# From the sixth chunk on, the second feed-forward product as seven block products, with streamed sums of weight blocks

## The chip, the core and the metric

One Trainium2 chip, one of its cores. A core has a matrix engine (TensorE, "PE" in the profile; its weight loads are listed apart as "PEld"), a vector engine (VectorE, "DVE"), a scalar engine (ScalarE, "ACT"), GpSimd ("POOL") and SyncE ("SP"), whose queue issues every transfer of this kernel. Working data lies in SBUF, on 128 partitions; products land in PSUM, which this kernel cuts into eight banks of 512 float32 columns. The metric is the device time of one launch in microseconds, here the median of three runs.

## The reference, cut to what matters

```python
# attention: q, k, v are (8 batches, 8 heads, 576, 64); 32 landmarks per head
q_lm, k_lm = means of q, k over 18 neighbouring rows
A, Bm, C = softmax(q k_lm'), softmax(q_lm k_lm'), softmax(q_lm k')
Z = inverse of Bm by six Newton steps
x = (A @ Z @ C @ v), heads side by side          # (8, 576, 512)
# feed-forward
u  = x + real(fft(fft(x, axis=1), axis=2))
un = (u - mean(u)) / sqrt(var(u) + 1e-6)         # per row of 512
out = u + np.maximum(un @ w_ch1, 0.0) @ w_ch2    # w_ch1 (512, 2048), w_ch2 (2048, 512)
```

The change touches the last product, `h @ w_ch2` with `h = max(un @ w_ch1, 0)`, for 8 x 576 = 4608 rows.

## The kernel before, in words

**Numbers in two halves.** Every large operand is split into a float16 high part and a float16 low part, "hi" and "lo". `mm3` makes one product of such pairs from three matmuls that add up in PSUM: hi x hi, hi x lo, lo x hi.

**Tiles and chunks.** The 4608 rows are 36 tiles of 128 rows. Attention works through eight batches; `mix` makes the tiles of a batch (four, or five with a tile shared by two batches), `norm` normalizes them, splits them and has them transposed by DMA into a buffer `unT`, which holds two tiles. Two tiles (256 rows) form a chunk, so there are 18 chunks, numbered 0 to 17. Tile `u` stays in a buffer of its own until its chunk is finished.

**A chunk** (`chunk`) loops over eight pairs of blocks of 128 hidden units; the prediction calls one such pass a group. In each group,
- the first product fills a bank `hp` with two blocks x 256 rows: 2 x 4 x 3 = 24 matmuls of 256 columns, stationary operand from `w1s`;
- ACT writes `h` hi as the ReLU of the bank, and DVE writes `h` lo;
- the second product adds to two banks `acc`, one per tile of 128 rows: 2 x 2 x 3 = 12 matmuls of 512 columns, stationary operand `h`, moving operand `w2s` (both weights stay in SBUF).

After the eighth group, DVE adds each `acc`, scaled by `inv2`, to its `u`, and SP stores `u`.

**The order of the work.** Operations are not issued as the Python code meets them. `Order` collects them with their dependences; `solve` plays them through with a price for each operation and writes an order for each engine. Among the operations that are ready and whose buffers are free, an engine takes the one with the lowest phase (`set`): -1 for the operations that turn `hp` into `h` and for the end of a chunk, 100 x the batch for attention, 1000 for the second product, 1001 for the first. So the first product fills PE's time when nothing else is ready. Consecutive matmuls between `together` and `apart` are one entry. A consumer on PE is planned a margin later than its operand is (0.8 us for the second product). On the chip each engine follows its list and waits on semaphores; each list is strictly in order, SP's too.

**Buffers** are pools with a number of slots, and those in `IN_ORDER` are given out in program order. The ones that matter are

```python
BANKS = {"at": 4, "h": 2, "acc": 2}
SLOTS = {"big": (1280, 8), ..., "u": (512, 7), "unT": (1024, 3), "h": (512, 4), "ws": (512, 3)}
```

(columns of float32, number of slots). `at` are attention's PSUM banks; `big` holds a batch's loads of q, k and v and its large intermediates; `ws` is a float32 work buffer of `weights`, which scales and splits both weights at the start.

In the profile nearly every operation has the line of the helper that issues them (1039), so operations are told apart by tile names: `hp<-unT,w` is the first product, `acc<-w,h` the second, `h<-hp` the ReLU and the low part, `u<-acc` the end of a chunk, `at<-...` attention's products, `big<-k_dram` a load, `unT<-row` a transposing DMA.

Of the kernel before, what the change touches and what calls it, by code (L numbers as in the profile page):

```python
# [10 lines left out]
F32 = mybir.dt.float32  # L11
F16 = mybir.dt.float16
# [3 lines left out]
AF = mybir.ActivationFunctionType  # L16
ALU = mybir.AluOpType
# [66 lines left out]
BANKS = {"at": 4, "h": 2, "acc": 2}  # L84
SLOTS = {"big": (1280, 8), "ml": (640, 3), "mt": (512, 5), "row": (528, 6), "u": (512, 7), "unT": (1024, 3), "h": (512, 4), "ws": (512, 3)}
# [20 lines left out]
class View:  # L106
# [42 lines left out]
    def box(self):  # L149
        if self.at_psum():  # L150
# [211 lines left out]
class Kernel:  # L362
    def __init__(self, ctx, tc, NB, q, k, v, w1, w2, t1, t1t, t2, diag, mask, out):
# [3 lines left out]
        pool = lambda n: ctx.enter_context(tc.tile_pool(name=n, bufs=1))  # L367
        self.pool, self.sm = pool("sb"), {}
        self.ps = ctx.enter_context(tc.tile_pool(name="ps", bufs=1, space=bass.MemoryType.PSUM))
        self.order = Order()  # L370
# [148 lines left out]
    def weights(self):  # L519
# [5 lines left out]
        s1, e1, s2, inv = (self.kept([P, n], F32, name) for n, name in ((4, "wsa"), (4, "wea"), (4, "wsb"), (1, "winv")))  # L525
        self.inv2 = inv
        for w in range(2):
            gram = self.new("acc")
            for f in range(NF):
# [3 lines left out]
                top, low = rv[:, :, 1], rv[:, :, 0]  # L533
                dst, mag = slots[w][f], low.bitcast(F32) if w else self.new("h")
                x = dst.bitcast(I32)
# [23 lines left out]
                if w == 0:  # L559
                    V.reciprocal(e1[:, g : g + 1], r)  # L560
                    V.tensor_scalar(s1[:, g : g + 1], r, 2.0**12, None, ALU.mult)
                else:
                    least = self.small(1, "wleast")
                    V.tensor_tensor(r, r, s1, ALU.mult)
                    V.tensor_reduce(least, r, AX.X, ALU.min)
                    V.tensor_scalar(s2, e1, least, 4.0, ALU.mult, ALU.mult)
                    V.reciprocal(inv, least)
                    V.tensor_scalar(inv, inv, 2.0**-13, None, ALU.mult)
                for f2 in range(NF) if w else range(4 * g, 4 * g + 4):
                    src, (hi, lo) = self.new("ws"), (hl[w][f2][:, y] for y in range(2))  # L570
# [8 lines left out]
    def load(self, b):  # L579
        res = []  # L580
        for g in range(2):
            kf, qf = self.big(), self.big()
            gs = slice(2 * g, 2 * g + 2)
            self.dma(kf[:, 0 : 2 * S].rearrange("p (r t) -> p r t", r=2), self.k[b, :, gs])
            self.dma(qf[:, 0 : 16 * SEG].rearrange("p (r t) -> p r t", r=2), self.q[b, :, gs])
            res.append([kf, qf])
        for g in range(2):
            vf = self.big()
            self.dma(vf.rearrange("p (c d) -> p c d", c=5), self.v[b, g].rearrange("(c p) d -> p c d", p=P))
            res[g].append(vf)  # L590
        return res

    def attention(self, b):
# [3 lines left out]
        self.set(10 * b if b == 0 else 100 * b, b, 0.1 if b == 0 else 0.4 if b == 1 else 1.0)  # L597
        loads = self.load(b)
        if b == 0:
            self.later()  # L600
# [36 lines left out]
        for g in range(2):  # L637
            qs = loads[g][1][:, 0:NQ].rearrange("p (x t) -> p x t", t=2 * SEG)
            for t, a, w in ((qm[g], 1, 128), (qr[g], 129, 16)):
                split(  # L640
                    *(t[:, y].rearrange("p r (s t) -> p (r s) t", t=w) for y in range(2)),
                    qs[:, :, a : a + w], sc[:, g : g + 1],
                )
        scr = self.small(1, "scr")
        for g in range(2):
# [77 lines left out]
    def landmarks(self, b, loads, qbd, lm):  # L723
# [84 lines left out]
        for g in range(2):  # L808
# [7 lines left out]
            A.copy(ET[:, 0:4].rearrange("p t m -> p (t m)"), ps)  # L816
            ps = self.at()
            tr(ps[:64, 0:128], Ces[g][:, 512:576], self.ident)
            A.copy(ET[:64, 4], ps[:64, 0:128])
# [27 lines left out]
        for g in range(2):  # L847
            for i in blocks:
                mm(ps[i, 64 * g : 64 * g + 64], nrm[i, g, 0, :], RE[i, g, 32:])
            for i, rows in enumerate(blocks):  # L850
                o, r = i % 2, i // 2
# [133 lines left out]
    def chunk(self, ch):  # L985
# [4 lines left out]
        for i in range(NF // 2):  # L990
            self.set(1001, -1, 0.3)
            ps = self.new("hp")
            for x in range(2):
# [4 lines left out]
                self.apart()  # L998
            if ch == 0 and i < 4:
                t = self.mid(512)  # L1000
            else:
                t = self.new("h")
            h = t.bitcast(F16).rearrange("p (y x t) -> p y x t", y=2, x=2)
# [13 lines left out]
        for t in range(TCH):  # L1017
            u = self.utiles[TCH * ch + t]
            V.scalar_tensor_tensor(u, acc[t], self.inv2, u, ALU.mult, ALU.add)
            self.dma(self.out[(TCH * ch + t) * P : (TCH * ch + t + 1) * P, :], u)  # L1020

    def run(self):
        self.ntile, self.utiles, self.unT = 0, [], []
        chunks = 0
        for b in range(self.NB):
# [81 lines left out]
```

## Time and profile before

| | |
|---|---|
| runs | 1051.32, 1051.76, 1053.48 us; median 1051.76 us |
| profiled execution | 1050.58 us; its span, first to last instruction, 1048.4 us |
| mean granted TensorE clock | 0.974 |
| PE busy | 982.3 us of the span |
| DVE, ACT, POOL busy | 592.7, 341.8, 191.7 us |
| first product | 3456 matmuls of 256 columns |
| second product | 1728 matmuls of 512 columns by the code, of which the trace recorded 1680 with `h` as the operand and 48 of chunk 0 with `mt` |
| chunk 4 ends, chunk 5 ends | stores begin at 417.15 and 460.14 us |

Rows of groups read: line, engine, operation, output<-inputs, shapes, xcount | busy us, mean ns of one | idle time of the engine just before, and who ended it. Rows of the timeline read: start us, length us, engine, what, xcount merged, and the idle time before with its releaser in brackets. Rows of stretches give the busy time of each engine, in brackets the instructions, then the granted clock, the share of the DMA engines and GB/s. Matmuls overlap, so the mean length of a matmul is not the time that it costs; distances between starts are.

### The profile page before, as it was taken

Reading aid. Unit: us, or ns where it says so; the run is one execution under the profiler, and the core shown is the slowest. Engines: PE = TensorE matmul, PEld = TensorE weight load, DVE = VectorE, ACT = ScalarE, POOL = GpSimd, SP = SyncE. Lnnn points to the kernel's source line nnn. Section 1 sums busy time; section 2 is a strip of 40 time slices with the busy share of each in tenths; the row PEclk is TensorE's granted clock in tenths of the full one; section 3 lists DMA queues with packets and bytes.
Section 4 is the critical chain, followed back from the end, with each engine's and each line's share of the span. In section 5 each row is a group of like instructions: output and inputs, shape, how many; then the busy total and the mean of one; then the engine's idle time right before and its main releaser. Section 6 shows DMA issues by size and latency. Waiting matters only on the chain.

```text
span 1048.4 us, 21403 instructions
## 1 busy us (share of the span) xinstructions
PE 982.3 (94%) x8922; PEld 665.0 (63%) x8922; DVE 592.7 (57%) x1558; ACT 341.8 (33%) x749; POOL 191.7 (18%) x199
## 2 busy tenths in 40 slices
PE   4664879999999999999999999999999999999998
PEld 3444735666666666766676676667666666667674
DVE  6999997995968752246744774178415243131111
ACT  4567553453524431123421442045212121111110
POOL 2458443033122100101110221021102000010000
PEclk9686989999999999999999999999999999999999
DMA  9656402325015200115110501051111100020000
GB/s 343 197 198 183 137 1 51 135 52 184 12 45 162 36 11 11 31 31 172 27 29 26 167 14 41 21 160 26 42 31 21 32 1 26 16 51 21 1 21 21
DMA packets 90992, 72.99 MB, mean 70 GB/s; under 512 B 61328, under 2 KB 79760, under 8 KB 90768
## 3 DMA queue, kind: packets, MB, share of 16 engines
q1 hardware_dynamic: 90896, 71.63, 22.4%
q8 instruction: 70, 1.15, 0.4%
q14 instruction: 26, 0.21, 0.1%
HBM read 48.02 MB, written 9.44 MB: 55 GB/s over the span
## 4 chain that ended last, share of the span: by engine, by line
PE 78%; DVE 16%; issue 2%; ACT 2%; POOL 1%; DMA 1%; SPq 0%; DVEq 0%; ACTq 0%; POOLq 0%
PE acc L1039 33%; PE hp L1039 32%; PE at L1039 13%; DVE w L1039 4%; DVE row L1039 2%; DVE big L1039 1%; DVE u L1039 1%; DVE ws L1039 1%; DVE Wx L1039 1%; DVE mt L1039 1%; DVE h L1039 1%; ACT Wx L1039 1%; DVE lm L1039 1%; DVE cmx L1039 1%; DMA big<-q_dram 1%
## 5 line engine op out<-in xcount | busy, mean ns | idle before, releaser
L1039 PE MATMUL hp<-unT,w 128*128 128x256 f16 x3456 | 400.7, 273 | 0.2 <-DVE h L1039 0.2
L1039 PEld LDWEIGHTS <-w 128*128 128x128 f16 (+1 forms) x3584 | 343.8, 98 | 81.0 <-DVE w L1039 19.2
L1039 PE MATMUL acc<-w,h 128*128 128x512 f16 x1680 | 384.2, 380 | 1.0 <-ACT h L1039 0.7
L1039 PEld LDWEIGHTS <-h 128*128 128x128 f16 x1680 | 160.4, 98 | 182.0 <-issue 6.3
L1039 DVE SCALAR_TENSOR_TENSOR h<-hp,h 128x512 f16<-128x512 f32 x140 | 96.4, 688 | 294.5 <-ACT h L1039 293.8
L1039 ACT ACTIVATE h<-hp 128x512 f16<-128x512 f32 x140 | 83.5, 596 | 387.4 <-PE hp L1039 378.9
L1039 POOL TENSOR_TENSOR r<-ve,mhalf 128x2 f32<-128x2 f32 (+1 forms) x20 | 14.4, 718 | 419.6 <-DVE ve L1039 397.9
L1039 DVE SCALAR_TENSOR_TENSOR u<-at,scw,row 128x128 f32<-128x128 f32 (+3 forms) x120 | 39.4, 387 | 32.2 <-PE at L1039 32.0
L1039 POOL TENSOR_TENSOR row<-row,row 128x512 f16<-128x512 f32 x36 | 45.1, 1265 | 38.8 <-ACT row L1039 38.8
L1039 PEld LDWEIGHTS <-mt 128*128 128x128 f16 x432 | 38.3, 100 | 17.8 <-issue 8.8
L1039 PEld LDWEIGHTS <-big 128*128 128x128 f16 (+1 forms) x768 | 40.4, 104 | 12.5 <-issue 6.5
L1039 DVE TENSOR_REDUCE lm<-big 128x32 f32<-128x576 f32 (+1 forms) x48 | 44.1, 942 | 5.9 <-DMA big<-k_dram 5.0
L1039 POOL TENSOR_TENSOR mt<-mt,asum 128x512 f32<-128x512 f32 x14 | 14.5, 1047 | 165.0 <-DVE asum L1039 163.7
L1039 POOL TENSOR_TENSOR w<-ws,w 128x512 f16<-128x512 f32 x24 | 33.0, 1392 | 18.3 <-ACT w L1039 18.3
L1039 DVE SCALAR_TENSOR_TENSOR u<-acc,winv,u 128x512 f32<-128x512 f32 x36 | 27.0, 750 | 14.7 <-PE acc L1039 14.7
L1039 PE MATMUL at<-big,qbd 128*64 128x288 f32 x128 | 22.5, 481 | 12.1 <-DVE qbd L1039 11.7
L1039 ACT ACTIVATE big<-big 128x1168 f16<-128x1168 f32 (+1 forms) x26 | 25.5, 984 | 25.5 <-DMA big<-q_dram 13.8
L1039 PE MATMUL at<-ml,big 128*128 128x262 f16 (+1 forms) x288 | 32.3, 284 | 0.7 <-DVE u L1039 0.6
L1039 ACT CAST row<-row 128x512 f16<-128x512 f32 x36 | 21.6, 616 | 32.4 <-DVE row L1039 26.3
L1039 DVE TENSOR_TENSOR mt<-mt 128x256 f32<-128x256 f32 x48 | 28.4, 609 | 5.7 <-PE at L1039 3.6
L1039 PE MATMUL acc<-w 128*128 128x128 bf16 x128 | 13.7, 245 | 19.0 <-DVE w L1039 16.4
L1039 PE MATMUL at<-RE 32*32 32x96 f32 (+1 forms) x768 | 26.2, 254 | 5.6 <-DVE RE L1039 5.6
(165 smaller groups left out, 982.1 us busy)
## 6 DMA issues: line engine op xcount, KB each, us to landing
w<-w_dram SPq DMA_DIRECT2D x22, 512.0 KB, 5.6
big<-v_dram SPq DMA_DIRECT2D x16, 640.0 KB, 9.2
big<-q_dram SPq DMA_DIRECT2D x16, 584.0 KB, 6.2
big<-k_dram SPq DMA_DIRECT2D x16, 576.0 KB, 4.8
out_dram<-u SPq DMA_DIRECT2D x36, 256.0 KB, 2.0
big<-w_dram SPq DMA_DIRECT2D x10, 512.0 KB, 6.9
unT<-row SPq DMA_TRANSPOSE x72, 2.4
t<-t_dram SPq DMA_DIRECT2D x1, 1048.0 KB, 9.9
```

The lines of the kernel that those rows point to most:

```text
L1039: getattr(engine, name)(*map(real, args), **{k: real(x) for k, x in kw.items()})
```

## The change

Chunks 0 to 4 stay as they are; chunks 5 to 17 (13 of 18) go through a new function `seven`.

In a group the second product multiplies a block matrix of 2 x 2 (two tiles of rows by two blocks of hidden units, each 128 x 128) with one of 2 x 2 (two blocks of hidden units by two halves of 256 output columns). `chunk` takes eight block products for that; `seven` takes Strassen's seven, each on sums or differences of blocks of both sides.

- *Left factors.* ACT writes the ReLU as float32 into `r` (a `ws` buffer). Two of the seven factors are blocks of `r` themselves: ACT copies their high parts to `h`, DVE subtracts for the low parts. The other five are sums and differences, made by three DVE operations into `c` (a new pool `sum`, 2 slots); ACT copies the high parts of all five (640 columns) to `h`, and POOL subtracts for the low parts (640 columns). `h` grows to 896 columns and has 3 slots.
- *Right factors.* Four of the seven are kept in SBUF: b11 and b22 as they were, and b12 - b22 and b21 - b11, which are written over b12 and b21 after chunk 4 (`differences_of`). Three (b11 + b22, b11 + b12, b21 + b22) are made once after chunk 3 (`sums_of`, 24 blocks), stored to device memory as 128 KB each, and loaded again in every group of every later chunk: 3 loads a group, 312 in all, into a ring of ten places in two `big` buffers that are held to the end.
- *Products.* Seven `mm3` of 256 columns, 21 matmuls instead of 12 of 512. The seven sums go to seven half banks: the two `acc` and two banks that are taken from `at` and held to the end.
- *End of a chunk.* DVE puts the seven sums together into the two `u`: two operations of 512 columns and eight of 256, instead of two of 512.
- *Room for it.* `unT` has 2 slots instead of 3. From the third batch on (`LATE`) v is loaded after the high and low parts of q are made. One bundle of attention's matmuls is cut in two, and the claim of `ET` is repeated for its second part, so that two `at` banks suffice. The scales of the weights are halved and doubled, so that sums of blocks stay in range.

```diff
-SLOTS = {"big": (1280, 8), ..., "unT": (1024, 3), "h": (512, 4), "ws": (512, 3)}
-IN_ORDER = ("big", "ml", "mt", "unT", "h", "ws", "hp", "acc")
+SLOTS = {"big": (1280, 8), ..., "unT": (1024, 2), "h": (896, 3), "ws": (512, 3), "sum": (640, 2)}
+IN_ORDER = ("big", "ml", "mt", "unT", "h", "ws", "sum", "hp", "acc")
+SEVEN, RING, LATE = 5, 10, 2
...
+    def block(self, n, a, b, op, out=None):
+        add = (self.G if n % 2 else self.V).tensor_tensor
+        t = self.new("ws")
+        add(t.rearrange("p (y d) -> p y d", y=2), a, b, op)
+        x = t[:, 0:256]
+        add(x, x, t[:, 256:512], ALU.add)
+        hl = t[:, 256:512].bitcast(F16).rearrange("p (y d) -> p y d", y=2) if out is None else out
+        self.A.copy(hl[:, 0], x)
+        self.G.tensor_tensor(hl[:, 1], x, hl[:, 0], ALU.subtract)
+        if out is None:
+            m = self.dram.tile([P, 256], F32, name=f"sums{len(self.sums)}")
...
+            self.dma(self.sums[-1], t[:, 256:512])
...
+    def seven(self, ch):
...
+        if ch == SEVEN:
+            self.held_banks = [self.new("at") for _ in range(2)]
+            self.ring = [self.new("big") for _ in range(2)]
...
+        acc = [self.new("acc") for t in range(TCH)] + self.held_banks
+        half = lambda k: acc[k // 2][:, 256 * (k % 2) : 256 * (k % 2) + 256]
+        for i in range(NF // 2):
+            (b11, b12), (b21, b22) = self.halves(i)
+            units = []
+            self.set(1000, -1)
+            for j in range(3):
...
+                self.dma(to, self.sums[3 * i + j])
...
+            self.set(1001, -1, 0.3)
+            ps = self.new("hp")
...
+            self.set(-1, -1)
+            r, c = self.new("ws"), self.new("sum")
+            h = self.new("h").bitcast(F16).rearrange("p (y k t) -> p y k t", y=2, k=7)
+            A.activation(r, ps, AF.Relu)
+            ones = r.rearrange("p (k t) -> p k t", k=4)[:, 0:4:3]
+            A.copy(h[:, 0, 0:2], ones)
+            rx = r.rearrange("p (x u t) -> p x u t", x=2, u=2)
+            V.tensor_tensor(c[:, 0:256], r[:, 0:256], r[:, 256:512], ALU.add)
+            V.tensor_tensor(c[:, 256:512].rearrange("p (x t) -> p x t", x=2), rx[:, :, 1], rx[:, :, 0], ALU.subtract)
+            V.tensor_tensor(c[:, 512:640], r[:, 0:128], r[:, 384:512], ALU.add)
+            V.tensor_tensor(h[:, 1, 0:2], ones, h[:, 0, 0:2], ALU.subtract)
+            cv = c.rearrange("p (k t) -> p k t", k=5)
+            A.copy(h[:, 0, 2:7], cv)
+            G.tensor_tensor(h[:, 1, 2:7], cv, h[:, 0, 2:7], ALU.subtract)
+            self.set(1000, -1, 0.8)
+            for to, k, w in ((0, 1, b21), (1, 0, b12), (2, 2, b22), (3, 3, b11), (6, 4, units[1]), (5, 5, units[2]), (4, 6, units[0])):
+                self.together()
+                mm3(half(to), lambda y: h[:, y, k], lambda y: w[:, y], start=(i == 0 and to in (0, 2, 5, 6)), stop=(i == NF // 2 - 1))
+                self.apart()
+        self.set(-1, -1)
+        u0, u1 = self.utiles[TCH * ch : TCH * ch + 2]
+        for u in (u0, u1):
+            V.scalar_tensor_tensor(u, acc[0], self.inv2, u, ALU.mult, ALU.add)
+        for k, plus, less in ((2, (u0, 1), (u0, 0)), (3, (u1, 0), (u1, 1)), (6, (u1, 1), None), (5, None, (u0, 0)), (4, (u0, 0), None), (4, (u1, 1), None)):
+            for to, scale in ((plus, self.inv2), (less, self.ninv2)):
+                if to:
+                    part = to[0][:, 256 * to[1] : 256 * to[1] + 256]
+                    V.scalar_tensor_tensor(part, half(k), scale, part, ALU.mult, ALU.add)
...
     def run(self):
...
-                self.chunk(chunks)
+                (self.seven if chunks >= SEVEN else self.chunk)(chunks)
                 chunks += 1
+                if chunks == SEVEN - 1:
+                    for i in range(NF // 2):
+                        self.sums_of(i)
+                elif chunks == SEVEN:
+                    for i in range(NF // 2):
+                        self.differences_of(i)
```

More of the change, by code (lines that the diff above doesn't have):

```diff
@@ L84 @@
 BANKS = {"at": 4, "h": 2, "acc": 2}
-SLOTS = {"big": (1280, 8), "ml": (640, 3), "mt": (512, 5), "row": (528, 6), "u": (512, 7), "unT": (1024, 3), "h": (512, 4), "ws": (512, 3)}
-IN_ORDER = ("big", "ml", "mt", "unT", "h", "ws", "hp", "acc")
+SLOTS = {"big": (1280, 8), "ml": (640, 3), "mt": (512, 5), "row": (528, 6), "u": (512, 7), "unT": (1024, 2), "h": (896, 3), "ws": (512, 3), "sum": (640, 2)}
+IN_ORDER = ("big", "ml", "mt", "unT", "h", "ws", "sum", "hp", "acc")
 LINK, PATIENCE = 0.05, 0.0
+SEVEN, RING, LATE = 5, 10, 2
 XP, LP = ((1, 1, 1, 1), (1, 1, 1, 1)), ((1, 1, 1, 1), (1, 0, 1, 0))
@@ L149, in box @@
     def box(self):
-        if self.at_psum():
+        if self.ap.space in (bass.MemoryType.PSUM, bass.MemoryType.DRAM):
             return 0, P, 0, 1 << 20
@@ L533, in weights @@
                 top, low = rv[:, :, 1], rv[:, :, 0]
-                dst, mag = slots[w][f], low.bitcast(F32) if w else self.new("h")
+                dst, mag = slots[w][f], low.bitcast(F32) if w else self.new("h")[:, 0:512]
                 x = dst.bitcast(I32)
@@ L586, in load, with load_v @@
             res.append([kf, qf])
+        return res
+    def load_v(self, b, loads):
         for g in range(2):
@@ L589, in load @@
             self.dma(vf.rearrange("p (c d) -> p c d", c=5), self.v[b, g].rearrange("(c p) d -> p c d", p=P))
[L590 to L591 removed]
+            loads[g].append(vf)
     def attention(self, b):
@@ L598, in attention @@
         loads = self.load(b)
+        if b < LATE:
+            self.load_v(b, loads)
         if b == 0:
@@ L643, in attention @@
                 )
+        if b >= LATE:
+            self.load_v(b, loads)
         scr = self.small(1, "scr")
@@ L817, in landmarks @@
             ps = self.at()
+            self.order.claim(ET)
             tr(ps[:64, 0:128], Ces[g][:, 512:576], self.ident)
@@ L849, in landmarks @@
                 mm(ps[i, 64 * g : 64 * g + 64], nrm[i, g, 0, :], RE[i, g, 32:])
+        self.apart()
+        self.together()
+        for g in range(2):
             for i, rows in enumerate(blocks):
@@ L998, in chunk @@
                 self.apart()
[L999 to L1002, printed above, removed]
+            t = self.mid(512) if ch == 0 and i < 4 else self.new("h")[:, 0:512]
             h = t.bitcast(F16).rearrange("p (y x t) -> p y x t", y=2, x=2)
@@ L1020, in chunk, with halves @@
             self.dma(self.out[(TCH * ch + t) * P : (TCH * ch + t + 1) * P, :], u)
+    def halves(self, i):
+        return [[self.w2s[2 * i + x][:, :, 256 * d : 256 * d + 256] for d in range(2)] for x in range(2)]
+    def block(self, n, a, b, op, out=None):
[9 more added lines that the diff above has]
+            m = self.dram.tile([P, 256], F32, name=f"sums{len(self.sums)}")
+            tile_ = Tile(Pool([m], False, kept=True))
+            tile_.slot = 0
+            self.sums.append(View(tile_, m))
+            self.dma(self.sums[-1], t[:, 256:512])
@@ L1022, in run @@
     def run(self):
+        self.unit, self.sums = 0, []
         self.ntile, self.utiles, self.unT = 0, [], []
```

36 lines of the change are left out of this document (33 added, 3 removed).

## The prediction

> **What bounds the kernel now.** I read the page first: busy times, then the chain that ended last.
>
> ```profile
> span 1048.4 us, 21403 instructions
> ...
> PE 982.3 (94%) x8922; PEld 665.0 (63%) x8922; DVE 592.7 (57%) x1558; ACT 341.8 (33%) x749; POOL 191.7 (18%) x199
> ...
> GB/s 343 197 198 183 137 1 51 135 52 184 12 45 162 36 11 11 31 31 172 27 29 26 167 14 41 21 160 26 42 31 21 32 1 26 16 51 21 1 21 21
> ...
> PE 78%; DVE 16%; issue 2%; ACT 2%; POOL 1%; DMA 1%; SPq 0%; DVEq 0%; ACTq 0%; POOLq 0%
> ```
>
> PE carries 78% of the chain, but a share over the whole span mixes stages. The view of stretches cuts it at 417 us, where the fifth chunk ends (chunk 4, counted from 0) and the changed ones would begin, and at 925 us, where attention is over.
>
> ```profile
> core 0: us, PE busy (x) PEld busy (x) DVE busy (x) ACT busy (x) POOL busy (x), PEclk, DMA share, GB/s
> 100.00:417.00 317.00, 302.98 (x3160) 203.38 (x3158) 238.31 (x648) 133.11 (x305) 75.51 (x77) 0.98 0.25 72
> 417.00:925.00 508.00, 507.68 (x4379) 344.67 (x4378) 241.37 (x651) 134.79 (x294) 62.87 (x65) 1.00 0.17 49
> 925.00:1003.00 78.00, 78.00 (x547) 53.28 (x545) 15.68 (x29) 10.79 (x18) 3.09 (x3) 1.00 0.07 18
> ```
>
> From 417 us on PE is idle for 0.3 us of 508, at a granted clock of 1.00; DVE works 241 of 508. What the change touches is a stage where only PE sets the time, so matmul time taken out there is worth its full length, as long as PE stays fed. The busy PE need not be PE at its best rate, so I take rates from the chain in time order, between starts in the pure feed-forward tail, and the weight loads from the groups of that stretch:
>
> ```profile
> 996.58 5.24 PE hp L1039 x48
> 1001.82 5.18 PE acc L1039 x24
> ```
> ```profile
> L1039 PEld LDWEIGHTS <-w 128*128 128x128 f16 x643 | 62.9, 98 | 10.3
> L1039 PEld LDWEIGHTS <-h 128*128 128x128 f16 x320 | 31.3, 98 | 35.0
> ```
>
> A 256-column product costs 5.24/48 = 109.2 ns, a 512-column one 5.18/24 = 215.8 ns. A pair of f-blocks (one i, a "group" below) takes 24 and 12 of them: 5.21 us, 41.7 us a chunk.
>
> **The change, part by part.**
>
> *The second product.* Per group 12 products of 512 columns (2.590 us) become 7 x 3 of 256 columns, each with its own 128-column weight load. The nearest row for that form is the first product: also 256 columns, one load each, 109.2 ns. 21 x 109.2 = 2.293 us, saving 0.297 us per group (less than an eighth, as two 256-column products cost 218.4 against 215.8). Thirteen chunks of eight groups are 104: **-30.9 us**. Bounds: half of a 512-column product, 107.9 ns, gives -33.7; no reason excludes a loss, and with the load of 98 ns left in the open 21 x 207 = 4.35 us would lose 1.76 us a group, 183 in all.
>
> On that the row stands first: 48 loads of 98 ns and 48 products fit into 5.24 us, so the load is hidden already. "TensorE: Matmul & The Clock Gate" in the Trainium skill, section "The mechanism", says loads overlap products in flight only when they target another row group; all of these are 128 rows deep. By that rule it would be the upper bound just given; the trace disagrees with it, and the sum goes by 109.2.
>
> *Making the seven left factors.* Today a group needs a ReLU on ACT and one subtraction on DVE, and the product starts soon after:
>
> ```profile
> 1006.84 5.40 PE L1039 MATMUL hp<-unT,w 128*128 128x256 f16 x48
> 1009.66 0.60 ACT L1039 ACTIVATE h<-hp 128x512 f16<-128x512 f32 x1 [7.20 <-PE hp L1039]
> 1010.28 0.69 DVE L1039 SCALAR_TENSOR_TENSOR h<-hp,h 128x512 f16<-128x512 f32 x1 [5.09 <-ACT h L1039]
> 1012.08 5.34 PE L1039 MATMUL acc<-w,h 128*128 128x512 f16 x24
> ```
>
> The factors are ready at 1010.97, 1.1 us before they are used. Prices of the new operations, from the nearest forms:
>
> ```profile
> L1039 DVE TENSOR_TENSOR mt<-mt x48: 390/421/1379, 34.3 to 799.3; 128x256 f32<-128x256 f32 x48
> ```
> ```profile
> L1039 DVE SCALAR_TENSOR_TENSOR u<-acc,winv,u 128x512 f32<-128x512 f32 x36 | 27.0, 750 | 14.7 <-PE acc L1039 14.7
> L1039 DVE SCALAR_TENSOR_TENSOR u<-at,scw,row 128x256 f32<-128x256 f32 x32 | 15.1, 478 | 28.1 <-PE at L1039 28.1
> L1039 DVE TENSOR_TENSOR RE<-RE,at 128x128 f32<-128x128 f32 x48 | 13.4, 280 | 14.8 <-ACT RE L1039 9.9 <-PE at L1039 4.6
> ```
> ```profile
> L1039 ACT CAST row<-row 128x512 f16<-128x512 f32 x36 | 21.6, 616 | 32.4 <-DVE row L1039 26.3 <-POOL row L1039 3.8 <-DVE cb L1039 1.1
> L1039 ACT ACTIVATE ml<-at 128x262 f16<-128x262 f32 x32 | 11.5, 388 | 9.8 <-PE at L1039 9.8
> ```
> ```profile
> L1039 POOL TENSOR_TENSOR row<-row,row x36: 1151/1182/1650, 79.9 to 931.7; 128x512 f16<-128x512 f32 x36
> ```
>
> Per group: ACT 0.60 as before, plus 0.39 (256 columns) plus 0.616 x 1.25 = 0.77; DVE three of 256 (0.42 each) and one of 128 (0.28) = 1.54 instead of 0.69; POOL 1.18 x 1.25 = 1.5 from nothing. In line: ReLU 0.6, three additions 1.1, copy 0.8, POOL 1.5, some 0.3 of hand-overs: 4.3 us from hp to the last factor, where 1.3 stood. Hidden if PE runs two first products (5.2 us) ahead; hp has 2 banks, h 3 slots, so it can, with 0.9 us to spare. Engine loads in 417 to 925 us, which holds 80 such groups and 11 chunk ends: DVE 241 + 80 x 0.85 + 42 (below) = 351 of about 485 us, 72%; ACT 135 + 93 = 228, 47%; POOL 63 + 120 = 183, 38%. None becomes the bound on paper. But DVE and POOL are not independent:
>
> ```profile
> 236.79 2.45 POOL L1039 TENSOR_TENSOR row<-mt,row 128x512 f16<-128x512 f32 x2
> ```
> ```profile
> 237.51 2.01 DVE L1039 TENSOR_TENSOR mt<-mt 128x256 f32<-128x256 f32 x2
> ```
>
> Two additions that take 0.42 each lasted 2.01 us and ended 0.3 us after POOL's pair. Every group now has four such DVE operations and one such POOL operation. I charge PE a wait of 0.06 us per group, x 104 = **+6 us**; bounds 0 (the cushion of 0.9 holds) and 0.5 us per group (52 us, the rival below). I take a value near the lower end because DVE is free 28% of the time and the planner ranks these DVE operations above attention.
>
> *The end of a chunk.* Two 512-column operations (1.5 us) become two and eight of 256: 1.5 + 8 x 0.478 = 5.3 us. They hold the accumulators, and queued behind them on DVE are the additions of the next chunk's first groups, for which PE then waits. PE has two first products (5.2 us) to run meanwhile. I take 0.4 us for each of 12 boundaries, **+5 us**; bounds 0 and 3.8 x 12 = 46.
>
> *The very end* is in the open. Now:
>
> ```profile
> 1043.37 0.75 DVE L1039 SCALAR_TENSOR_TENSOR u<-acc,winv,u 128x512 f32<-128x512 f32 x1 [1.13 <-PE acc L1039]
> ...
> 1044.66 0.75 DVE L1039 SCALAR_TENSOR_TENSOR u<-acc,winv,u 128x512 f32<-128x512 f32 x1 [0.55 <-PE acc L1039]
> ```
>
> After: 5.3 us of DVE that can begin only when the first accumulator is whole, some 1.6 us before PE's end, so 3.7 instead of 0.8 follow it: **+3 us** (bounds 2 and 6, with the longer chain of the last group).
>
> *Streaming the sums.* 312 loads of 128 KB, 393 KB per group of 4.91 us: 80 GB/s on top of 49, where the first slice moved 343. On SP three issues a group; behind one that waits for its slot (the products ten blocks back) stand the transposes, attention's loads and the stores.
>
> ```profile
> big<-v_dram SPq DMA_DIRECT2D x16, 640.0 KB, 9.2
> ...
> out_dram<-u SPq DMA_DIRECT2D x36, 256.0 KB, 2.0
> ```
>
> A ring of ten is 3.3 groups, 16 us, against 2.0 us alone and 9.2 behind a batch of loads. Cost 0; without that cover one late block per attention batch costs up to 9 us, x 5 = 45.
>
> *Making the sums and differences.* 40 blocks, half added up on DVE (512 and 256 columns, some 0.84 + 0.42 each: 25 us), half on POOL (1.2 + 0.6: 36 us), then 40 copies on ACT and 40 subtractions of 0.6 us on POOL. They lie in 100 to 460 us; in 100 to 417 DVE has 79 us free and POOL 241. Taken as 0, high end 10. The doubled and halved scales cost nothing.
>
> *Fewer buffers.* Attention keeps two of its four PSUM banks, six of eight big buffers (so v loads later), unT two of three, h three of four. In the stretch of interest attention's bank work is:
>
> ```profile
> 417.00:925.00 508.00, 88.91 (x1470) 22.18 (x792) 81.07 (x238) 44.71 (x135) 1.00 0.17 49
> ```
>
> Written and read one after the other that is 89 + 81 + 45 = 215 us of one bank; doubled for waits and for pairs taken together, 430 of the 970 bank-microseconds that two banks have. And attention has a lead:
>
> ```profile
> 876.93 1.63 SPq L1039 DMA_DIRECT2D out_dram<-u  x2
> 889.28 5.12 SPq L1039 DMA_TRANSPOSE unT<-row  x4
> 919.92 1.63 SPq L1039 DMA_DIRECT2D out_dram<-u  x2
> ```
>
> A chunk's store at 877 frees the u buffers; 12.4 us later the transposes of tiles 31 and 32 begin, issued by 894, 26 us before the chunk that needs tile 31 starts (at the next store, 920). Late attention eats that lead before PE waits. Cost 0; high end 50 (rival).
>
> **Sum.** -30.9 + 6 + 5 + 3 = -17 on the span of 1048.4: 1031.5. The profiled execution took 1050.58, 2.2 around its span, and the median of the runs is 1.2 above that: **1035 us**.
>
> **Rivals.**
> 1. *Nothing is lost* but the very end: 1051.8 - 30.9 + 3 = 1024. For it: PE idle 0.3 us of 508 under the same planner. Against: a chain of 4.3 us instead of 1.3.
> 2. *PE waits for the factors* (other side). Place: POOL's subtraction of a group meets DVE's additions of the next. If the 1.5 us of POOL beat the 0.9 us cushion by 0.5 in every group, 104 x 0.5 = 52, and 1051.8 - 28 + 52 = 1076. It decides from 28/104 = 0.27 us per group on. For it: 2.01 us for two additions, a mean of such rows (609 ns) well above their median. "SBUF — State Buffer" in the Trainium skill, section "Who interferes with whom", has a DVE instruction with two SBUF inputs and a GpSimd one that reads SBUF exclude each other for a whole instruction; the row above agrees. Against: first products can be run ahead.
> 3. *Two banks starve attention*: the lead of 26 us is used up and PE waits some 10 us in each of five batches: 1051.8 - 28 + 50 = 1074; it decides at 28 us in all. Against it: 430 of 970.
> 4. *Losses just eat the gain*: 1047 to 1056, boundaries and ring at the middle of their bounds.
>
> **Numbers.** Chances: forecast (1027 to 1047) 0.52, rival 1 0.18, rival 2 0.13, rival 3 0.09, rival 4 0.08. About 0.2% (2.1 us) is what a measurement of this kernel tells from no change. Faster 0.52 + 0.18 + 0.02 of rival 4 = 0.72; same 0.04 of rival 4 and 0.02 from the mild ends of rivals 2 and 3, 0.06; slower the other 0.20 of these two and 0.02 of rival 4, 0.22. The range runs from 1021, the full 30.9, to 1060, leaving out the greater part of rivals 2 and 3; without the slower cases it is 1022 to 1047.
>
> **What would show it.** Right: acc products of 256 columns at 109 ns between starts in the chain; a pure feed-forward chunk at 39 to 40 us between stores instead of 41.7; PE idle under 3% after the fifth chunk; some 5.3 us of DVE at chunk ends; ring loads landing within 10 us. Wrong: PE waits on POOL or DVE for h above 0.27 us a group (rival 2), on at or unT in attention's stretch (rival 3), on DMA for the ring, or acc products well off 109 ns.

## The result, and the profile after

The changed kernel takes 1064.49 us (median of 4 runs, 1063.26 to 1066.13) against 1052.22 for the kernel before on the same chip (4 runs, 1051.32 to 1053.48): a ratio of 1.0117, with a 95% interval of 1.0097 to 1.0137 (in brackets behind the ratios below). The forecast was 1035. The profiled execution took 1063.53, with a span of 1061.7 us against 1048.4 (+13.3) and a mean granted clock of 0.959 against 0.974.

From the page of the changed kernel: span, busy times, chain, POOL's part of the left factors, and the ring's loads.

```profile
span 1061.7 us, 24997 instructions
...
PE 963.6 (91%) x9858; PEld 758.3 (71%) x9858; DVE 780.1 (73%) x2015; ACT 466.3 (44%) x997; POOL 420.5 (40%) x383
...
PE 39%; DVE 28%; issue 15%; POOL 8%; ACT 5%; DMA 4%; SPq 1%; POOLq 0%; DVEq 0%; ACTq 0%
...
L1149 POOL TENSOR_TENSOR h<-sum,h 128x640 f16<-128x640 f32 x104 | 148.7, 1432 | 329.3 <-ACT h L1149 304.1
...
big<-sums SPq DMA_DIRECT2D x312, 128.0 KB, 2.1
```

PE's busy time fell by 18.7 us (982.3 to 963.6) and yet the span grew: PE now waits. Its share of the chain falls from 78% to 39%, DVE's rises from 16% to 28%. The stretches say where (start:end and length, then busy time of PE, PEld, DVE, ACT and POOL with instructions, granted clock, DMA share, GB/s):

```profile
200.00:300.00 100.00, 92.62 (x918) 62.36 (x916) 87.20 (x246) 43.88 (x109) 50.44 (x55) 0.97 0.36 104
417.00:925.00 508.00, 485.30 (x5074) 407.28 (x5073) 373.13 (x971) 220.04 (x463) 190.25 (x155) 1.00 0.37 107
475.00:903.00 428.00, 405.50 (x4338) 339.11 (x4336) 325.18 (x855) 189.99 (x403) 155.79 (x124) 1.00 0.37 111
925.00:1003.00 78.00, 78.00 (x717) 69.91 (x715) 37.89 (x95) 28.36 (x50) 25.91 (x20) 1.00 0.38 107
```

While attention runs beside the changed chunks, PE is idle for 22.7 us of 508, where it was idle for 0.3; in the pure tail it is never idle. The stores, one pair at the end of each chunk, split the loss further; first the kernel before (chunks 4 and 17), then the changed one (chunks 4, 14 and 17):

```profile
417.15 1.63 SPq L1039 DMA_DIRECT2D out_dram<-u  x2
...
1044.15 1.63 SPq L1039 DMA_DIRECT2D out_dram<-u  x2
```
```profile
429.54 2.19 SPq L1149 DMA_DIRECT2D out_dram<-u  x2
...
941.14 0.81 SPq L1149 DMA_DIRECT2D out_dram<-u  x2
...
1058.13 0.81 SPq L1149 DMA_DIRECT2D out_dram<-u  x2
```

- 12.4 us are lost before the first changed chunk begins (429.54 against 417.15).
- From chunk 4's store to the span's end it takes 632.2 us, against 631.3: thirteen chunks of seven products gained nothing.
- In the tail the gain is there: chunks 15 to 17 take 1058.13 - 941.14 = 117.0 us against 1044.15 - 919.92 = 124.2, 2.41 us a chunk. The forecast had 8 x 0.297 = 2.38.

Who is waited for shows in PE's waits from 430 us to the end (waiting engine and tile, releaser: us in total, times, longest):

```profile
PE at L1149 <- DVE Wx L1149: 7.5, 3, 2.8
PE at L1149 <- ACT ml L1149: 4.7, 6, 1.1
PE acc L1149 <- DVE h L1149: 2.4, 4, 1.6
PE at L1149 <- DVE big L1149: 1.9, 1, 1.9
PE at L1149 <- DVE RE L1149: 1.6, 2, 0.9
PE hp L1149 <- ACT ws L1149: 1.4, 1, 1.4
PE acc L1149 <- POOL h L1149: 1.3, 2, 1.1
PE at L1149 <- DVE u L1149: 1.3, 4, 0.5
PE acc L1149 <- DVE u L1149: 0.7, 1, 0.7
...
```

17.9 us stand at `at`, with three small rows of 0.9 us that aren't shown, and 5.8 at `acc` and `hp`. Three of the seven sums also lie in `at` banks (their products read `at<-big,h`), but the timeline puts every one of these `at` waits at a product of attention. What makes DVE late is to be seen in the order of time:

```profile
489.50 2.70 POOL L1149 TENSOR_TENSOR row<-row,row 128x512 f16<-128x512 f32 x2 [2.81 <-ACT row L1149]
...
491.12 2.44 DVE L1149 TENSOR_TENSOR sum<-ws 128x256 f32<-128x256 f32 x3
...
493.95 0.61 PE L1149 MATMUL acc<-w,h 128*128 128x256 f16 x4 [1.64 <-DVE h L1149]
...
498.41 1.40 POOL L1149 TENSOR_TENSOR h<-sum,h 128x640 f16<-128x640 f32 x1 [1.32 <-ACT h L1149]
...
498.93 1.70 DVE L1149 TENSOR_TENSOR sum<-ws 128x256 f32<-128x256 f32 x3 [1.02 <-ACT ws L1149]
...
500.66 0.72 ACT L1149 CAST h<-sum 128x640 f16<-128x640 f32 x1 [1.40 <-DVE sum L1149]
501.29 0.89 ACT L1149 ACTIVATE big<-at 128x320 f16<-128x320 f32 x2
...
501.85 0.92 DVE L1149 SCALAR_TENSOR_TENSOR big<-at,big 128x320 f16<-128x320 f32 x2 [0.88 <-ACT big L1149]
502.42 1.57 PE L1149 MATMUL at<-t,mt 128*128 128x160 f16 x12 [1.94 <-DVE big L1149]
...
1051.31 0.96 DVE L1149 TENSOR_TENSOR sum<-ws 128x256 f32<-128x256 f32 x3 [4.27 <-ACT ws L1149]
```

A group's three additions take 0.96 us when POOL is idle (last line) and 2.44 us beside POOL's subtractions of `row`, which the kernel before has too; the product that needs the factors waits 1.64 us. Beside the new subtraction of a group at 498.41 they take 1.70 us. ACT waits 1.40 us for them, and only then comes to an operation of attention that stands behind in its list; DVE waits 0.88 us for that one, and a product of attention 1.94 us. So a delay of the factors is handed down the lists to attention.

### The profile page after: what moved, and what is told of

It is laid out like the page before. It is cut to its first block, busy times and chain, and to the rows that moved or that the text cites. A ratio compares the mean times of both kernels' runs of the same rounds, so it can differ in the third digit from the quotient of the medians.

```text
span 1061.7 us, 24997 instructions
## 1 busy us (share of the span) xinstructions
PE 963.6 (91%) x9858; PEld 758.3 (71%) x9858; DVE 780.1 (73%) x2015; ACT 466.3 (44%) x997; POOL 420.5 (40%) x383
## 4 chain that ended last, share of the span: by engine, by line
PE 39%; DVE 28%; issue 15%; POOL 8%; ACT 5%; DMA 4%; SPq 1%; POOLq 0%; DVEq 0%; ACTq 0%
PE hp L1149 15%; PE at L1149 14%; PE acc L1149 10%; DVE sum L1149 5%; POOL h L1149 5%; DVE u L1149 3%; DVE w L1149 3%; DVE row L1149 2%; DVE mt L1149 2%; DVE h L1149 1%; DVE ws L1149 1%; ACT h L1149 1%; SPq L1149 1%; DVE Wx L1149 1%; ACT ws L1149 1%
## 5 line engine op out<-in xcount | busy, mean ns | idle before, releaser
L1149 PEld LDWEIGHTS <-h 128*128 128x128 f16 x2616 | 248.7, 98 | 85.0 <-issue 9.2
L1149 POOL TENSOR_TENSOR h<-sum,h 128x640 f16<-128x640 f32 x104 | 148.7, 1432 | 329.3 <-ACT h L1149 304.1
L1149 PE MATMUL acc<-w,h 128*128 128x256 f16 (+1 forms) x1680 | 270.0, 300 | 5.7 <-DVE h L1149 2.4
L1149 DVE TENSOR_TENSOR sum<-ws 128x256 f32<-128x256 f32 (+1 forms) x312 | 141.9, 506 | 133.7 <-ACT ws L1149 126.9
L1149 ACT CAST h<-sum 128x640 f16<-128x640 f32 x104 | 75.4, 725 | 109.6 <-DVE sum L1149 108.4
L1149 PE MATMUL at<-big,h 128*128 128x256 f16 x936 | 123.0, 274 | 0.0
L1149 ACT ACTIVATE ws<-hp 128x512 f32<-128x512 f32 x104 | 61.9, 595 | 136.4 <-PE hp L1149 135.7
L1149 POOL TENSOR_TENSOR w<-ws,w 128x512 f16<-128x512 f32 (+1 forms) x40 | 45.1, 1142 | 37.6 <-ACT w L1149 36.0
L1149 DVE TENSOR_TENSOR h<-ws,h 128x256 f16<-128x256 f32 x104 | 47.2, 454 | 0.0
L1149 ACT ACTIVATE h<-hp 128x512 f16<-128x512 f32 x36 | 21.5, 596 | 37.6 <-PE hp L1149 37.4
```

The source lines that it names most:

```text
L1149: getattr(engine, name)(*map(real, args), **{k: real(x) for k, x in kw.items()})
```

## Experiments

Each is an edit of the changed kernel, but for one of the kernel before, and timed beside the kernel before. My theory after the result: POOL's subtraction in each group delays DVE's operations, those of attention too, under an order that was planned without that delay. Rivals: too few banks and buffers; streaming; making the sums; an order that is bad by chance.

**POOL reads nothing in a group.** The five low parts that POOL subtracts become zeros, written twice so that POOL is busy about as long (2 x 0.63 us against 1.40); the planner sees the old price and gives the same order.

```diff
-            G.tensor_tensor(h[:, 1, 2:7], cv, h[:, 0, 2:7], ALU.subtract)
+            lo = h[:, 1, 2:7]
+            self.order.op("POOL", 0.15 + 2.1e-3 * 640, 0.05, [lo], [cv, h[:, 0, 2:7]], (self.nc.gpsimd, "memset", (lo, 0.0), {}))
+            self.order.ops[-1].calls.append((self.nc.gpsimd, "memset", (lo, 0.0), {}))
```

> The changed kernel with the same order of work on every engine; only POOL's subtraction of 640 columns is put by two fills of the same place with zeros (about as long, but reading nothing from SBUF), so the low parts of five of the seven left factors are left out. Theory A (DVE's additions, with two SBUF operands, and POOL's subtraction shut each other out, and the fixed order hands the delay to PE): DVE's additions fall from 506 ns to 390-420, the 22 us that PE idles between 475 and 903 us shrink to under 8, and the time is 1040 to 1048 us. Theory B (two PSUM banks and fewer buffers hold attention up): additions faster as well, but PE idle stays near 20 us and the time within 4 us of 1064.

1046.18 us, ratio 0.9952 (0.9935 to 0.9968). Chunk 4 ends where it did (429.34), so all the difference lies behind it: 613.2 us from there to the span's end, 19.0 less (18.3 by the medians: the profiled execution is the fastest of this run's four). The additions from 475 to 903 us, one row each of the changed kernel and of this one (busy us, mean ns of one):

```profile
L1149 DVE TENSOR_TENSOR sum<-ws 128x256 f32<-128x256 f32 x129 | 74.7, 616 | 40.4 <-ACT ws L1149 35.0 <-POOL h L1149 2.6 <-ACT RE L1149 1.5
```
```profile
L1151 DVE TENSOR_TENSOR sum<-ws 128x256 f32<-128x256 f32 x138 | 61.9, 487 | 47.0 <-ACT ws L1151 46.7
```
```profile
475.00:903.00 428.00, 419.80 (x4503) 354.84 (x4501) 309.01 (x889) 197.98 (x417) 146.86 (x197) 1.00 0.39 115
```

More additions, each 129 ns shorter, and PE idle for 8.2 us in this stretch instead of 22.5. POOL's part per group is also some 0.14 us shorter, which this run doesn't separate. PE's waits at attention's products from 430 us on fall from 17.9 to 6.8 us.

**Smaller buffers alone**: `unT` 2, `h` 3, v loaded late, but every chunk as before, no sums, nothing held.

```diff
-                (self.seven if chunks >= SEVEN else self.chunk)(chunks)
+                self.chunk(chunks)
...
-                if chunks == SEVEN - 1:
-                    for i in range(NF // 2):
-                        self.sums_of(i)
...
```

> The changed kernel with eight plain block products in every chunk, no sums of weights made or streamed, no banks or big buffers held: what is left of the change is unT with 2 slots, h with 3 larger ones, the later load of v and the cut bundles of attention. Theory B: chunk 4 ends some 12 us later than before, at 426 to 431 us instead of 417, and the time is 1060 to 1066 us. Theory A says nothing on this stage; if the 12 us come from making the sums of the weights on DVE and POOL instead, chunk 4 ends at 416 to 420 us and the time is 1051 to 1055 us.

1054.73 us, 1.0023 (1.0013 to 1.0032). Chunk 4's store begins at 420.04, 2.9 us late; from there to the span's end 630.8 us, as before. A small cost, and all of it early.

**The held banks and ring added**, chunks still as before.

```diff
+            if ch == SEVEN and i == 0:
+                self.set(1000, -1)
+                for _ in range(2):
+                    ring = self.new("big")
+                    self.dma(ring[:, 0:256], self.v[0, 0, 0:128])
+                    ring.tile.left += 1
...
+            if ch == SEVEN and i == 0:
+                self.order.claim(*(self.new("at") for _ in range(2)))
...
-                (self.seven if chunks >= SEVEN else self.chunk)(chunks)
+                self.chunk(chunks)
```

> As the kernel with small buffers and plain products, and from chunk 5 on two of attention's four PSUM banks and two of the eight big buffers are held without use. Theory B: PE idles 15 to 25 us more between chunk 4's end and 925 us than without the held buffers, and the time is 15 to 25 us above it. Theory A: PE idle under 4 us in that stretch and the time within 4 us of the kernel without the held buffers.

1059.7 us, 1.0072 (1.0057 to 1.0087). From chunk 4's store to the span's end 637.1 us, 6.3 more than without holding.

```profile
475.00:903.00 428.00, 424.03 (x3784) 286.34 (x3782) 220.33 (x592) 120.51 (x267) 56.08 (x59) 1.00 0.19 52
```

PE is idle for 4.0 us of this stretch. Held together, two banks and two big buffers do starve attention a little, by an eighth of the 50 us that the third rival had; which of the two does it, the run doesn't separate.

**Only the last four chunks take seven products.**

```diff
-SEVEN, RING, LATE = 5, 10, 2
+SEVEN, RING, LATE = 14, 10, 2
```

> The changed kernel with the seven products only from chunk 14 on, where attention is nearly done; small buffers and making of sums as in the changed kernel. Both theories: four chunks save some 2.4 us each, 39 instead of 41.7 us between stores, less 3 at the very end. Theory A, and B with the cost of the small buffers at the start: 1052 + 12 - 7 = 1055 to 1060 us. If the small buffers cost nothing: 1044 to 1048 us.

1055.56 us, 1.0032 (1.002 to 1.0044). The stores of the chunk ahead of the four and of the last one:

```profile
891.33 1.63 SPq L1149 DMA_DIRECT2D out_dram<-u  x2
...
1051.81 0.82 SPq L1149 DMA_DIRECT2D out_dram<-u  x2
```

That is 160.5 us for four chunks against 1044.15 - 876.93 = 167.2 before, a gain of 6.7 (4 x 2.38 = 9.5 forecast); but the chunk ahead of them ends 14.4 us later than before, though it is an old chunk. 13.3 of these are there at chunk 4 (430.49 against 417.15), from the smaller buffers and the sums.

**Additions that read one operand from PSUM.** DVE reads `hp` itself for one side, so that it has one operand in SBUF. The whole computation.

```diff
-            V.tensor_tensor(c[:, 0:256], r[:, 0:256], r[:, 256:512], ALU.add)
...
+            stt = lambda out, a, b, op: V.scalar_tensor_tensor(out, a, 0.0, b, ALU.max, op)
+            stt(c[:, 0:256], ps[:, 0:256], r[:, 256:512], ALU.add)
...
```

> The changed kernel, whole computation, with DVE's four operations of a group taking one operand from PSUM (the ReLU redone on the way) and only the other from SBUF; POOL's subtraction is as it was. The order is planned anew. Theory A (DVE operations with two SBUF operands and POOL's reads shut each other out): the four operations keep a steady length near 0.48 and 0.34 us, with no rows above 0.6; PE idles under 10 us between chunk 4's end and 903 us, and the time is 1044 to 1052 us, near the 1046 of the kernel whose POOL doesn't read. If POOL's load or the length of the chain matters instead: within 5 us of 1064.

1057.5 us, 1.0054 (1.0034 to 1.0075). From 475 to 903 us, durations as min/median/max in ns, first in the changed kernel, then in this one:

```profile
L1149 DVE TENSOR_TENSOR sum<-ws x194: 271/414/1653, 474.8 to 899.3; 128x256 f32<-128x256 f32 x129, 128x128 f32<-128x128 f32 x65
```
```profile
L1150 DVE SCALAR_TENSOR_TENSOR sum<-hp,ws x196: 271/414/426, 474.7 to 897.2; 128x256 f32<-128x256 f32 x130, 128x128 f32<-128x128 f32 x66
```
```profile
475.00:903.00 428.00, 412.12 (x4409) 346.56 (x4407) 301.89 (x869) 192.51 (x406) 149.78 (x126) 1.00 0.39 112
```

The delay of these operations is gone, none above 426 ns where 1653 stood. The Trainium skill, page "SBUF — State Buffer", section "Who interferes with whom", has a DVE instruction with at most one SBUF input, outside its two-port modes, not contending with GpSimd, and one with two SBUF inputs not contending with a GpSimd instruction that only writes: the first agrees with this row, the second with the shorter mean beside the zeros above. Yet only 7.0 us come back of the 18.3 of the first experiment (PE idle 15.9 us from 475 to 903). PE's waits from 430 us on say why (the changed kernel's stand above):

```profile
PE hp L1150 <- DVE h L1150: 8.5, 5, 2.5
PE at L1150 <- ACT ml L1150: 2.3, 2, 1.1
PE at L1150 <- DVE Wx L1150: 1.9, 2, 1.5
PE at L1150 <- DVE RE L1150: 1.7, 1, 1.7
...
PE at L1150 <- DVE kbd L1150: 1.0, 1, 1.0
...
PE at L1150 <- DVE ml L1150: 0.5, 1, 0.5
...
```

The waits at attention's products fall from 17.9 to 7.4 us, nearly as far as with the zeros (6.8). But the first product now waits 8.5 us for DVE to let go of a bank `hp`, which DVE reads itself here; the changed kernel has no such wait. So 7.0 us is not the share of the factors' delay: the edit brings a cost of its own. That attention waits less than half as long, although POOL still reads and attention's own DVE operations are still slow (one of them, `klm<-lm,sc,klm`, took 263 ns in the mean before, 593 in the changed kernel, 270 with the zeros, 628 here), points to the delay of the factors' operations as what mostly held attention up. The order was planned anew, so the split is not exact.

**A higher price in the plan.** One number of the planner: a DVE `tensor_tensor` with both operands in SBUF counts 2.1 ns a column instead of 1.4, for 256 columns 0.07 + 0.54 = 0.61 us, the mean measured beside POOL, instead of 0.43, the undisturbed duration. The instructions are the same.

```diff
-                rate = 1.4e-3
+                rate = 2.1e-3
```

> The changed kernel with one number of the planner changed: DVE operations on two SBUF operands are priced at 2.1 instead of 1.4 ns a column, near their measured mean, so that consumers are planned later. Operations and their lengths are the same. If the loss is the fixed order's ignorance of the delays, the time is 1048 to 1056 us; if it is the blocked DVE time itself, 1060 to 1066 us.

1040.91 us, 0.9899 (0.9885 to 0.9914): 23.6 us less than the change, and faster than the kernel before. Chunk 4's store begins at 418.73 (10.8 earlier), the rest takes 619.4 us (12.8 less).

```profile
L1149 DVE TENSOR_TENSOR sum<-ws x198: 276/418/1620, 480.3 to 897.7; 128x256 f32<-128x256 f32 x132, 128x128 f32<-128x128 f32 x66
```
```profile
475.00:903.00 428.00, 417.83 (x4461) 351.49 (x4460) 330.85 (x867) 191.26 (x405) 157.36 (x128) 1.00 0.39 114
```

The delays are as long as they were, up to 1620 ns; PE is idle for 10.2 us instead of 22.5. That other work now stands ahead of what is late is my reading; no run takes it apart.

**No streaming.** 302 of the 312 ring loads are left out; later groups multiply by what lies in the ring.

```diff
-                self.dma(to, self.sums[3 * i + j])
+                if self.unit <= RING:
+                    self.dma(to, self.sums[3 * i + j])
```

> The changed kernel with the ring filled once: 302 of the 312 loads of sums are left out, and later groups multiply by what the ring holds. Theory A: streaming is hidden, time 1061 to 1066 us. Theory C (loads of the sums come late, or their issues on SP hold up transposes and attention's loads): 1045 to 1057 us.

1067.06 us, 1.0156 (1.0136 to 1.0177): no gain. The streams are hidden.

**The sums aren't made.** A copy of a block is stored instead of each of the 24 streamed sums.

```diff
+        if out is None:
+            self.A.copy(hl, a)
+        else:
...
```

> The changed kernel with the 24 sums of weight blocks not made: an ACT copy of one block is stored in their place, so 12 pairs of additions on DVE, 12 on POOL and 24 subtractions on POOL are left out before chunk 5. If making the sums is what delays the stage before chunk 5 (chunk 4 ended at 429.5 us with it and at 420 in the kernel without sums and with small buffers): chunk 4 ends at 418 to 423 us and the time is 1053 to 1058 us. If not: 1062 to 1066 us.

1059.7 us, 1.0075 (1.0056 to 1.0094). Chunk 4's store begins at 420.47, 9.1 us earlier; some is given back later, the total is 4.8 less. The stretches where the sums are made, first before, then without them:

```profile
100.00:200.00 100.00, 89.79 (x880) 59.53 (x878) 87.50 (x196) 50.43 (x107) 36.15 (x35) 0.95 0.30 96
200.00:300.00 100.00, 96.62 (x1116) 65.84 (x1115) 82.74 (x260) 45.33 (x108) 25.16 (x27) 1.00 0.24 68
```
```profile
200.00:300.00 100.00, 97.43 (x1130) 66.93 (x1128) 83.05 (x265) 46.27 (x110) 23.84 (x26) 1.00 0.31 88
```

With the sums (the changed kernel's row at the top) POOL works 50.44 us of 200 to 300 instead of 23.84, and PE 92.62 at a clock of 0.97 instead of 97.43 at 1.00. DVE is at 87 and 83 of 100 before the change already. Whether POOL's half of the sums or DVE's does the harm these runs don't separate.

**The price on the kernel before, and both remedies together.**

```diff
-                rate = 1.4e-3
+                rate = 2.1e-3
```

> The kernel before, with the planner's price for DVE operations on two SBUF operands at 2.1 instead of 1.4 ns a column, the edit that brought the changed kernel from 1064 to 1041 us. If the price repairs what the seven products brought in (theory A): 1049 to 1055 us, no gain to speak of. If it repairs the kernel's order in general, and the gain isn't the seven products': 1030 to 1042 us.

> The changed kernel with both: the price of 2.1 ns, and DVE's four operations of a group with one operand from PSUM. If delays by POOL and the order's ignorance of them are one loss, the two don't add up: 1038 to 1046 us, since the first-product bank is held longer. If they add: below 1036 us.

The kernel before gains 3.4 us by the price: 1048.36, 0.9965 (0.9952 to 0.9978). Price and PSUM operands together on the change: 1040.88, 0.99 (0.9883 to 0.9916), as with the price alone. That the second remedy adds nothing doesn't say what it would be worth alone, since PE waits 4.3 us for the banks `hp` again. With the same price on both sides the seven products are worth some 7 us (1048.36 to 1040.91), not 30.9 and not -12. And before chunk 5 the price repairs most: chunk 4's store begins at 414.51 in the kernel before with the price and at 418.73 in the changed one, 4.2 us apart instead of 12.4.

**Sums later, and longer margins.** With the price, the sums can't begin before chunk 1 is over; in another run, without it, the margins of the second product (0.8 to 1.6 us) and of attention from the fourth batch on (1.0 to 2.0) are doubled.

```diff
+        if out is None:
+            self.order.ops[-1].before[self.ended] = None
...
+                if chunks == 1 + 1:
+                    self.ended = self.order.ops[-1]
```
```diff
-        self.set(10 * b if b == 0 else 100 * b, b, 0.1 if b == 0 else 0.4 if b == 1 else 1.0)
+        self.set(10 * b if b == 0 else 100 * b, b, 0.1 if b == 0 else 0.4 if b == 1 else 1.0 if b == 2 else 2.0)
...
-            self.set(1000, -1, 0.8)
+            self.set(1000, -1, 1.6)
```

> The changed kernel with the price of 2.1 ns, and the sums of weight blocks made only after chunk 1, some 240 us, out of the stretch in which DVE is busiest. If making them costs PE time only because DVE is short there: chunk 4 ends 3 to 8 us earlier than 419 and the time is 1033 to 1038 us. If it costs the same anywhere: 1039 to 1043 us.

> The changed kernel with old prices, but PE's consumers planned later by a fixed margin: 1.6 instead of 0.8 us for the second product, 2.0 instead of 1.0 us for attention from batch 3 on. If the loss is that PE's list comes to operations whose operands are late: 1046 to 1056 us. If DVE's order matters (attention's own chain on DVE and POOL): 1058 to 1066 us.

1041.78 (0.9904, 0.989 to 0.9919) and 1060.2 (1.0084, 1.006 to 1.0108). Later sums bring nothing: chunk 4's store begins at 420.3, where 3 to 8 us before 419 had been expected. Doubled margins bring 4.3 us of the price's 23.6: room on PE's side alone is not what the plan lacks.

**Is it the price, or a lucky order?** Two orders from another hand-over price (`LINK` 0.06 and 0.04 instead of 0.05), a price in between, and the price together with POOL's zeros.

```diff
-LINK, PATIENCE = 0.05, 0.0
+LINK, PATIENCE = 0.06, 0.0
```
```diff
-                rate = 1.4e-3
+                rate = 1.8e-3
```

> The changed kernel with old prices and one harmless number of the planner moved: the hand-over between operations is 0.06 instead of 0.05 us, which makes another order with no knowledge of the delays. If the changed kernel's loss is systematic: 1058 to 1068 us. If the changed kernel's order was an unlucky one: below 1052 us.

> As the kernel with the moved hand-over, but 0.04 instead of 0.05 us: a second order without knowledge of the delays. If the loss is systematic: 1058 to 1068 us. If orders scatter: below 1052 us.

> The changed kernel with the price of DVE operations on two SBUF operands at 1.8 ns a column, between 1.4 (1064 us) and 2.1 (1041 us). If the price works by planning for the measured delays, the time lies between, 1042 to 1056 us. If the two orders differ by chance, anywhere from 1040 to 1066.

> The changed kernel with the price of 2.1 ns, in its order, and POOL's subtraction of 640 columns put by two fills with zeros (low parts of five left factors left out). If planning for the delays takes away only the waits on late operands and the blocked time of DVE still costs: 1028 to 1036 us. If the price already takes away all that POOL's reads cost: 1038 to 1042 us.

The two other orders take 1060.73 (1.0083, 1.0066 to 1.0099) and 1064.19 (1.0116, 1.0101 to 1.0131): with the low price the loss stays. Three plans with the price of 2.1 (alone, with PSUM operands, with later sums) took 1040.91, 1040.88 and 1041.78, so it isn't one lucky order either. But the price of 1.8 gives 1062.05 (1.0096, 1.008 to 1.0113), a miss of the 1042 to 1056 expected: the gain does not grow with the price but comes somewhere between 1.8 and 2.1; why there stays open. The price with POOL's zeros gives 1029.07 (0.9784, 0.977 to 0.9799):

```profile
475.00:903.00 428.00, 425.22 (x4565) 360.64 (x4563) 308.30 (x883) 197.41 (x415) 149.16 (x203) 1.00 0.40 116
```

PE is idle for 2.8 us there, and 11.8 us beyond the price alone come back: the better order covers a part of the delay only.

**Where the price counts**: only for the operations inside `seven`, or only for the others.

```diff
+PRICE = [1.4e-3]
...
-                rate = 1.4e-3
+                rate = PRICE[0]
...
+        PRICE[0] = 2.1e-3
...
+        PRICE[0] = 1.4e-3
```

> The changed kernel with the price of 2.1 ns for the DVE operations of the new function alone; those of attention and of the weights at the start are priced at 1.4 as before. Until chunk 4's end the order is that of the changed kernel, so 428 to 431 us there. If the loss after it is in the additions of the seven factors being later than planned: 1048 to 1054 us. If it is in attention's own operations: 1060 to 1066.

> The other half: 2.1 ns everywhere but in the new function, where the price is 1.4. Chunk 4 ends at 417 to 421 us, as with the price everywhere. If the loss after it is in the additions of the seven factors: 632 us more, 1050 to 1056 us. If it is in attention's own operations: 1040 to 1044 us.

Inside alone 1058.14 (8 runs, 1052.7 to 1062.62; 1.0053, 1.0032 to 1.0073), outside alone 1050.86 (10 runs, 1047.62 to 1053.32; 0.9988, 0.9977 to 1.0). The gains over the change, 6.3 and 13.6, make 20 of the 23.6, but they lie in different places. Priced outside, the profiled execution begins chunk 4's store at 418.94, 10.6 us earlier, and then takes 632.6 us to the span's end, no less than the 632.2 of the changed kernel. Priced inside, it begins that store at 430.84, no earlier, and then takes 625.6 us, 6.6 less. So the larger gain is made before any factor exists. Behind chunk 4 the price of attention's operations alone brings nothing, that of the factors alone 6.6 us, and both together 12.8. These runs scatter more than the others; the profiled execution with the price outside is 2.4 us above its median.

## Why the prediction was wrong, step by step

- *The second product*, -30.9: right where PE is kept fed, 2.41 us a chunk in the tail against 2.38. Behind chunk 4 as a whole, PE's busy time fell by 23.7 us only (626.3 to 602.7): an estimate with 109.2 and 215.8 ns a product leaves 86.4 us before and 93.1 after for the same 1470 products of attention. Where these 6.7 us come from was not found; with POOL's zeros it is 2.6. The rule of the Trainium skill ("TensorE: Matmul & The Clock Gate", section "The mechanism") by which the loads would stay in the open does not hold here either: PE is busy 78.00 of 78.00 us with 717 products and 715 loads, where 78 us at 109.2 ns hold 714.
- *Making the seven left factors*, +6: this step failed, by its size and by who pays. Since 30.9 - 3 - 6.3 us should have been gained behind chunk 4 and -0.9 was, some 22 us went here; 19.0 of them come back when POOL doesn't read. The row that carried it was quoted (two additions in 2.01 us), but the price was worked out for the product that needs the factors alone, with its cushion of 0.9 us. The delays that POOL's 104 reads of 1.4 us bring to DVE are handed on: PE waits 17.9 us at attention's products, against 5.8 at `hp` and `acc`. The second rival had the cause, the place (a group's subtraction meets the additions of the next) and the sign, but let PE wait for the factors. Its sign, waits on `h` above 0.27 us a group, did not show: they are 3.7 us in all, 0.04 a group. The loss as a whole, 22 us or 0.21 a group, also stayed below the size at which it was to decide by itself.
- *The argument "DVE is free 28% of the time and the planner ranks these operations above attention"* was the slip: ranked above attention, they push attention back. With the factors' operations undelayed (PSUM operands), attention's products wait 7.4 us instead of 17.9.
- *Making the sums*, 0 with a high end of 10: wrong, about 9 under this plan. The cover was read over 100 to 417 us (79 us of DVE free); from 100 to 300 us only 30 of 200 were. But short cover is not what the runs show as the cause: with the price of 2.1 chunk 4 ends 4.2 us later than before, of which the smaller buffers had 2.9 at the old price, and sums made after chunk 1 gained nothing.
- *Fewer buffers*, 0: 2.9 before chunk 5 and 6.3 by the held banks and ring, both measured with the old chunks.
- *Ends of chunks*, +5: too high. In the tail they cost nothing, and `acc` waits for `u` 0.7 us in all from 430 us on.
- *Streaming*, 0: right; 2.1 us to landing, and no gain without it.
- *The very end*, +3: about right, with two waits for the last factors (0.24 and 1.08 us) and 2.3 us of DVE behind PE:

```profile
1052.66 0.87 PE L1149 MATMUL acc<-w,h 128*128 128x256 f16 x6 [0.24 <-DVE h L1149]
...
1054.62 0.61 PE L1149 MATMUL acc<-w,h 128*128 128x256 f16 x4 [1.08 <-POOL h L1149]
...
1057.23 1.26 DVE L1149 SCALAR_TENSOR_TENSOR u<-at,winv,u 128x256 f32<-128x256 f32 x3
```

Put together on the span: -30.9 for the products, +3 at the very end, +2.9 and +6.3 for the buffers, +9.1 for the sums and 22 to 23 for DVE beside POOL make +12.4 to +13.4, where 13.3 was measured. The last term is what the others leave; 19.0 of it is measured by itself. Shown is that POOL's reads carry most of the loss behind chunk 4, and that the low price carries a good part of the loss on both sides of it; the two overlap, and what step of the plan turns between 1.8 and 2.1 ns was not found.

## What to carry to other kernels

Work moved from the engine that bounds to engines with free time is paid by whatever else waits in those engines' lists: ask who is queued behind it, not only who waits for its result. When an order is planned from prices, a duration that another engine stretches (here 415 ns alone, 616 in the mean) can be worth pricing with the stretching in it: that one number brought 23.6 us here, more than the change itself. It is to be tried, not trusted: a price of 1.8 ns, over half of the way from 1.4 to 2.1, brought only 2.4.

## What the hardware showed beyond what was expected

Beside reads by POOL a DVE addition with two SBUF operands took up to 1653 ns, in a row whose median is 414; with one operand in PSUM none took over 426, and beside zeros that POOL only writes the mean fell from 616 to 487 ns. And the granted clock fell in the changed kernel where PE had a gap, later than the gap (start:end, length, busy times, clock):

```profile
120.00:130.00 10.00, 4.54 (x35) 2.79 (x35) 9.04 (x15) 5.11 (x8) 2.81 (x3) 0.69 0.52 154
130.00:140.00 10.00, 8.19 (x76) 5.37 (x72) 7.37 (x38) 5.42 (x15) 1.76 (x2) 0.50 0.01 2
```

In the 10 us after a stretch in which PE worked 4.54, the clock was 0.50: here a gap of PE cost more than its length. With the smaller buffers alone the clock falls in the same place (0.72 and 0.77), so it is not the sums that bring it.
